# A spectral mixing layer with a routed feed-forward on one core: sine halves compared after the cosine rows, and one conditional store

## The chip, the cores and the metric

The kernel runs on one core of a Trainium2 chip. The metric is device microseconds of one execution. The kernel before takes 200.77 us, the median of three runs (200.58 to 201.01).

## The reference, cut to what matters

```python
x = A_x                                                   # 2048 tokens x 576, float32
h = x + _A_ref(_layernorm(x), seq_re, seq_im, hid_re, hid_im)
h2 = h + _B_ref(_layernorm(h), w_r, w_gate, w_up, w_down)

def _A_ref(x, dft_seq_re, dft_seq_im, dft_hid_re, dft_hid_im):
    a = jnp.einsum("bsd,ed->bse", x, dft_hid_re)
    b = jnp.einsum("bsd,ed->bse", x, dft_hid_im)
    return jnp.einsum("ts,bse->bte", dft_seq_re, a) - jnp.einsum("ts,bse->bte", dft_seq_im, b)

def _B_ref(x, w_r, w_gate, w_up, w_down):
    r = x @ w_r                                           # one score per token
    idx = jnp.argsort(-r, axis=-1)[:, :1]                 # the best token alone
    g, u = _silu(x_sel @ w_gate), x_sel @ w_up            # 576 -> 4608
    y = ((g * u) @ w_down) * _sigmoid(r_sel)              # 4608 -> 576
    return x + scatter(y at idx)
```

The two sequence matrices are 2048 x 2048 and arrive as inputs, as do the hidden matrices (576 x 576) and the three weights of the feed-forward (4608 x 576 each). Everything is float32. One token gets the feed-forward; all others get h plus its layer norm.

## The kernel before, in words

**Slots and tiles.** Token t lies on partition t // 16 in slot t mod 16, so X holds 16 slots of 128 x 576. A row of tiles of the cosine matrix (i = 0) or the sine matrix (i = 1) belongs to one slot j and is loaded as a tile of nine blocks of 128 x 128 (576 KB). Cosine and sine are symmetric, so the kernel multiplies with folded inputs and needs only the rows 0 to 8, in two groups: group zero of the list GROUPS is rows 1 to 5 (called group one in the change's title), the other is rows 6, 7, 0 and 8. Buffers: D0, D1 and D2 for the rows that are multiplied (five, five and four tiles), and a ring of seven tiles R, joined by the D tiles that are free at the time, for what is only compared.

**Comparisons.** Since the matrices are inputs, the kernel may only fold them if they really are symmetric. It reads the whole of both and compares. `off_h` (line 387) compares the two halves of each block of the rows in D, in two operations for each call; `off_s` (line 375) compares a tile with its mirrored part and `off_t` (line 380) a tile with that of row 16 - j. VectorE (DVE) writes the differences as bf16 into one of two slots of the buffer Q, ScalarE (ACT) squares and sums them (line 368), and at the end a sum that is not zero branches into a general version of the whole computation. With these inputs it is not taken. The mirrored parts come as gathers that GpSimd issues (POOL, line 301); all other loads are issued by SP in a fixed order (line 357 for the tiles, 403 and 405 for the hidden matrices W, 1173 and 1175 for the weights of the feed-forward). A load into a ring tile waits until the comparisons that read the tile's former content are done, and what stands behind it on its queue waits too.

**Around them.** PE multiplies the folded input XF with the rows in five blocks (line 565); ACT copies one part (579) and DVE keeps the result in Z (583). PE then multiplies Z with W (610), DVE adds the residual (619) and takes the router's score (623), ACT the variance (630). When all scores are there, the token is found, its slot is brought to all partitions, and the feed-forward runs as products and sums on POOL (1201), DVE (1190, 1197) and ACT (1206), with the last product on PE (1228). ACT stores the token's row last (1251).

**Stores of the other rows.** `STORE_RUNS` lists runs of slots (first slot, count) that POOL stores when the results of the batch that holds the run's first slot are there (lines 667 and 669). `LATE_RUNS` are two runs, slots 4 to 8 and slot 0, that SP stores under a condition, in two places (line 1052): early, behind the first feed-forward loads, if the token lies in one of those slots, and otherwise behind the last load. `other_rows` (lines 1040 to 1046) works out the two flags on POOL.

**What sets the order.** Python writes each step into a list with an engine, an estimated duration and the steps it depends on. `Plan.order` then runs through the list: at each point an engine takes, of the steps that are ready, the one with the longest way to the end. The instructions of each engine are emitted in that order, and an engine never departs from it. `qs.take()` hands out the two slots of Q in the order in which the steps are written down. In the part that the change touches, the order of writing is: halves of group zero in three portions (rows 1 and 2, rows 3 and 4, row 5), each with its cosine and sine tiles in one slot of Q and one square (2304, 2304 and 1152 elements wide); then `c_check` for cosine rows 1 to 5; then the five blocks on PE.

Of the kernel before, what the change touches and what calls it, by code (L numbers as in the profile page):

```python
# [7 lines left out]
F32 = mybir.dt.float32  # L8
# [3 lines left out]
OP = mybir.AluOpType  # L12
AX = mybir.AxisListType

P = 128
# [22 lines left out]
GROUPS = [[1, 2, 3, 4, 5], [6, 7, 0, 8]]  # L38
# [4 lines left out]

HALVES = [[(0, 2), (2, 2), (4, 1)], [(0, 2), (2, 2)]]

STORE_RUNS = [(1, 3), (13, 3), (11, 2), (9, 2)]
LATE_RUNS = [(4, 5), (0, 1)]

X_RUNS = [(0, 2), (14, 16), (2, 6), (6, 10), (10, 14)]

# [2 lines left out]
HM = P // 2  # L53
# [17 lines left out]
class Plan:  # L71
# [6 lines left out]
    def add(self, eng, dur, fn, *deps, tail=0.0, push=0.0):  # L78
        flat = []
        for d in deps:  # L80
            flat += d if isinstance(d, list) else [d]
        n = {"eng": eng, "dur": dur, "fn": fn, "deps": [d for d in flat if d], "tail": tail, "push": push}
        n["i"] = len(self.ops)
        self.ops.append(n)
        return n
# [57 lines left out]
def kernel(  # L143
# [13 lines left out]
    pe, act, dve, pool, sp = nc.tensor, nc.scalar, nc.vector, nc.gpsimd, nc.sync  # L157

    consts = ctx.enter_context(tc.tile_pool(name="consts", bufs=1))
    small = ctx.enter_context(tc.tile_pool(name="small", bufs=3))  # L160
# [132 lines left out]
    ov = out.rearrange("(p k) d -> p k d", k=NK)  # L293
# [11 lines left out]
    X = mp.tile([P, NK, D], F32, name="X")  # L305
# [10 lines left out]
    Q = QT.bitcast(BF16).rearrange("p (n w) -> p n w", n=2)  # L316
# [62 lines left out]
        o = Q[:, u % 2, 14 * P : QW].rearrange("p (k m) -> p k m", m=P)  # L379
        dve.tensor_tensor(o, C[NK - j, i, False], C[j, i, False][:, :, ::-1], op=SIGN[i])  # L380

    def off_h(g, c, n, i, u):

        o = Q[:, u % 2, i * 9 * n * HM : (i + 1) * 9 * n * HM].rearrange("p (c k m) -> p c k m", k=9, m=HM)
        t = DT[g, i][:, c : c + n]
        for k, op in enumerate((OP.subtract, OP.add)):
            dve.tensor_tensor(o[:, :, k::2, :], t[:, :, k::2, 0:HM], t[:, :, k::2, HM:P], op=op)  # L387
# [208 lines left out]
    def slots_of(j):  # L596
        return [j, NK - j] if j in PAIRS else [j]
# [86 lines left out]
    add = plan.add  # L684

    def then(f, *args):
        return lambda: f(*args)
# [20 lines left out]
    def in_turn(eng, f, mb, *deps):  # L708
        LAST[eng], d = load(eng, f, mb, LAST[eng], *deps)
        return d  # L710

    IDENT = []
    for k, n in X_LOADS:
        d = in_turn("SP" if k < 9 else "POOL", then(load_x, k, n), 0.295 * n)
# [11 lines left out]
    for a, b in X_RUNS:  # L726
# [4 lines left out]
        m = [add("ACT", 0.95, then(measure, k), f, push=push) for k, f in zip(ks, r)]  # L731
        o = add("POOL", 0.3, then(totals, a, b), e, m)
# [3 lines left out]
        o = add("POOL", 2.0, then(biases, a, b), r, o)  # L736
# [6 lines left out]
    users = {b: [] for b in ["XF", "Z", "Q", "WA", "WB", "WC", *range(N_RAW)]}  # L743
# [16 lines left out]
    for k in FOLDED:  # L760
        dg, use, at = [], [], []
        for sl in slots_of(k):
            n = next(places)
            UF[sl] = LATER[n]
            at.append(PLACE[n])
            if k in PAIRS:
                u, w = dgs.take()
                dg.append(add("DVE", 0.17, then(diag, sl, u), MEAS[sl], w, IDENT))
                use.append(u)
        if k in PAIRS:  # L770
            of = ys if k % 2 else zs
# [30 lines left out]
    CU = {}  # L802

    def c_load(j, i, mirror):
        CU[j, i, mirror] = ring("POOL" if mirror else "SP", load_c, 0.46 if mirror else 0.59, j, i, mirror)
# [8 lines left out]
            LAST["SP"], d = load("SP", then(load_c, None, j, i, False), 0.59, w, LAST["SP"])  # L814
            CU[j, i, False] = u, d

    def c_half(g, c, m):
        u, w = qs.take()
        cus = [[CU[j, i, False] for j in GROUPS[g][c : c + m]] for i in range(2)]
        n = [  # L820
            add("DVE", 0.16 + 0.62 * m, then(off_h, g, c, m, i, u), [d for _, d in cus[i]], w)
            for i in range(2)
        ]
        for i in range(2):
            for b, _ in cus[i]:
                users[b].append(n[i])
        squares(u, 9 * m * P, n)

    def squares(u, w, n, ps=P):
        SQUARES.append(add("ACT", 0.3 + w / 1200, then(square, u, w, ps), n))  # L830
        qs.users[u].append(SQUARES[-1])

    def c_check(j, i):

        u, w = qs.take()
        u0, d0 = CU[j, i, False]
        c_load(j, i, True)
        u1, d1 = CU[j, i, True]
        n = [add("DVE", 1.08, then(off_s, j, i, u, 0), d0, d1, w)]
        users[u0] += n  # L840
        users[u1] += n
        free.append(u1)
        if j in PAIRS:
            m = NK - j
            c_load(m, i, False)
            c_load(m, i, True)
            (u2, d2), (u3, d3) = CU[m, i, False], CU[m, i, True]
            n.append(add("DVE", 1.08, then(off_s, m, i, u, 1), d2, d3, w))
            users[u3].append(n[1])
            n.append(add("DVE", 1.36, then(off_t, j, i, u), d0, d2, w))  # L850
            users[u0].append(n[2])
            users[u2] += n[1:]
            free.extend([u3, u2])
        if u0[0] == "D1":
            free.append(u0)
        squares(u, QW if j in PAIRS else 7 * P, n)
# [28 lines left out]
    def seq_step(g, n):  # L885
        nonlocal pe_last
        w = len(GROUPS[g]) * HM
        (z0, w0_), (z1, w1_) = zs.take(), zs.take()
        need = [CU[j, i, False][1] for i in PARTS[n] for j in GROUPS[g]]
        pe_last = add("PE", 9 * w * 0.00171, then(seq, g, n), need, FOLDS, w0_, w1_, pe_last)  # L890
        for i in PARTS[n]:
            for c in range(len(GROUPS[g])):
                users[D_TAG[g, i], c].append(pe_last)
        users["XF"] = [pe_last]
        SEQ[g, n] = pe_last, z0, z1

    def keep_step(g, n):
        w = len(GROUPS[g]) * HM
        pe, z0, z1 = SEQ[g, n]
        u, wo = odds.take()  # L900
        h = add("ACT", 0.11 + 0.00085 * w, then(keep, g, n, 0), pe, wo)
        l = add("DVE", 2 * (0.07 + 0.00106 * w), then(keep, g, n, 1), h, ZU.get((g - 1, n > 0), []))
        odds.users[u].append(l)
        zs.users[z0].append(l)
        zs.users[z1].append(h)
        KEPT.setdefault(g, []).append(l)
# [22 lines left out]
    def batch(js):  # L929
# [6 lines left out]
        for k in [k for j in js for k in slots_of(j)]:  # L936
            if k in (0, 8):
                RESULTS.append(add("POOL", 1.3, then(result_on_pool, k), f, push=push + 5.0))
            else:
                RESULTS.append(add("ACT", 0.79, then(result, k), f, push=push))  # L940
        for k, n in STORE_RUNS:
            if k in [q for j in js for q in slots_of(j)]:
# [8 lines left out]
        for b in [b for b in free if type(b) is tuple and b[0] == tag]:  # L951
            free.remove(b)

    for c, m in HALVES[0]:
        c_half(0, c, m)
    for j in GROUPS[0][:3]:
        c_check(j, 0)
    w_first()
    for j in GROUPS[0][3:]:
        c_check(j, 0)  # L960
    for n in (0, 1, 4, 2, 3):
        seq_step(0, n)
        keep_step(0, n)
# [18 lines left out]
    for i in range(2):  # L982
        for j in GROUPS[1]:
            c_check(j, i)
    for c, m in HALVES[1]:
        c_half(1, c, m)
    for c in range(2):
        hid_step(0, c)
    for n in (0, 1):
# [12 lines left out]
    T = {}  # L1002
# [32 lines left out]

    def other_rows():

        s = small.tile([1, 3], F32, tag="near", name="near", bufs=1)
        T["late"] = small.tile([1, 2], I32, tag="late", name="late", bufs=1)
        pool.tensor_scalar(s[:, 0:1], T["ci"][0:1, 1:2], LATE_RUNS[0][0] - 0.5, None, op0=OP.is_ge)  # L1040
        pool.tensor_scalar(s[:, 1:2], T["ci"][0:1, 1:2], sum(LATE_RUNS[0]) - 0.5, None, op0=OP.is_le)
        pool.tensor_scalar(s[:, 2:3], T["ci"][0:1, 1:2], 0.5, None, op0=OP.is_le)
        pool.tensor_tensor(s[:, 0:1], s[:, 0:1], s[:, 1:2], op=OP.mult)
        pool.tensor_tensor(s[:, 0:1], s[:, 0:1], s[:, 2:3], op=OP.add)
        pool.tensor_scalar(T["late"][:, 0:1], s[:, 0:1], 1.0, 0.0, op0=OP.mult, op1=OP.add)
        pool.tensor_scalar(T["late"][:, 1:2], s[:, 0:1], -1.0, 1.0, op0=OP.mult, op1=OP.add)

    def store_if(n):

        on = sp.value_load(T["late"][0:1, n : n + 1], min_val=0, max_val=1)  # L1050
        for k, m in LATE_RUNS:
            st = sp.dma_start(ov[:, k : k + m, :], X[:, k : k + m, :], cond=on)
            tc.declare_no_dep(st.ins, group="spread", reason="stores of different rows")
            tc.add_to_no_dep_group("direct", st.ins)
            if n == 1:
                tc.declare_no_dep(st.ins, group="kept", reason="stores that only one of two conditions lets run")
                tc.add_to_no_dep_group("late", st.ins)
            else:
                tc.add_to_no_dep_group("kept", st.ins)

    def to_all():
        ph = T["ph"] = ypair("ph")
# [29 lines left out]
    rows = add("DVE", 0.55, T["steps"][4], most)  # L1092
# [3 lines left out]
    near = add("POOL", 1.0, other_rows, slot, push=50.0)  # L1096
# [26 lines left out]
    o = add("DVE", 1.0, check_sum, SCORES, SQUARES, xs_is)  # L1123
    o = add("PE", 0.3, check_all, o)
# [6 lines left out]
    for b in range(NJ // TW):  # L1131
        j = TW * b
# [112 lines left out]
    def late_part():  # L1245
        T["mv"] = nc.values_load(T["miss"][0:1, 0:1], min_val=0, max_val=1)
        store_if(1)
# [13 lines left out]
    def plan_ffn(after):  # L1261
# [41 lines left out]

        load_to(N_BUF)
        LAST["SP"] = add("SP", 1.5, then(store_if, 0), near, RESULTS, LAST["SP"])
        for b in range(NJ // TW):
            j = TW * b
# [23 lines left out]
    with tc.If(T["mv"], preferred_fallthrough_block=False):  # L1331
        with ExitStack() as gen:
# [33 lines left out]
            with ExitStack() as hs:  # L1366
# [9 lines left out]
                with tc.For_i(0, NK, 1) as k:  # L1376
                    dve.tensor_copy(xr, row_of(GX, k))
                    norm(xn, xr, "x")
                    for a in range(5):
                        w = min(P, D - a * P)  # L1380
# [4 lines left out]
                    for c in range(4):  # L1385
                        pa = zbank(f"gpa{c}")
                        for a in range(5):
                            w = min(P, D - a * P)
# [39 lines left out]
            key, ci = steps[5]()  # L1428
# [75 lines left out]
```

## Time and profile before

| | |
|---|---|
| median of three runs | 200.77 us |
| profiled execution | 201.27 us |
| its span | 199.2 us |
| DVE busy | 166.1 us (83%) |
| ACT busy | 140.5 us (71%) |
| PE busy | 130.4 us (65%) |
| POOL busy | 122.8 us (62%) |
| moved by DMA | 77.81 MB, mean 391 GB/s |

A row of a timeline gives start, duration, engine, line, operation, result<-inputs, how many instructions are merged in it (xN), and in brackets how long the engine stood idle before it and what ended that. A row of waits gives who waited for whom: microseconds in total, times, the longest. In a table of stretches each engine's busy time stands in its column, then the granted clock of PE, the mean busy share of the 16 DMA engines, and GB/s. The page's slices are 1/40 of the span, about 5 us each; a digit is the busy share in tenths.

### The profile page before, as it was taken

What the parts mean: (1) busy time and instruction counts of PE and PEld (TensorE: products, weight loads), DVE (VectorE), ACT (ScalarE), POOL (GpSimd) and SP (SyncE); (2) the same over time, 40 slices, a digit from 0 to 9 for tenths busy, and PEclk for the clock granted to TensorE, in tenths of its full rate; (3) what the DMA queues carried; (4) which work ended last, traced back from release to release, by engine and by line L of the source; (5) the groups of instructions that cost most, each with busy time, mean ns of one, the idle gap of its engine ahead of it and who ended that gap; (6) DMA issues with size and microseconds to landing.
All of it is one profiled execution on the core that took longest, in us unless ns stands there. A gap on an engine that the chain in (4) does not pass through costs nothing. (4 is left out here: it accounts for less than half of the span.)

```text
span 199.2 us, 2787 instructions
## 1 busy us (share of the span) xinstructions
PE 130.4 (65%) x758; PEld 89.9 (45%) x758; DVE 166.1 (83%) x419; ACT 140.5 (71%) x259; POOL 122.8 (62%) x134
## 2 busy tenths in 40 slices
PE   0007989999999989899999996600241444085840
PEld 0005667764767778677877774400121111043220
DVE  4389997989999859997999999999839997899410
ACT  2298863783987794799587599997629999786400
POOL 6578888495528878998870000006439999998500
PEclk9999999999999999999999999985555555555798
DMA  5999999999979999999999999999999999999991
GB/s 190 361 418 415 411 411 409 409 372 346 402 275 366 415 398 391 404 407 412 407 401 418 420 420 422 427 414 423 422 428 425 428 422 420 431 420 412 422 387 42
DMA packets 14491, 77.81 MB, mean 391 GB/s; under 512 B 1855, under 2 KB 1859, under 8 KB 11143
## 3 DMA queue, kind: packets, MB, share of 16 engines
q1 hardware_dynamic: 10463, 56.56, 70.8%
q0 software_dynamic: 4000, 21.03, 26.3%
q8 instruction: 7, 0.11, 0.2%
q14 instruction: 13, 0.11, 0.1%
q10 hardware_dynamic: 8, 0.00, 0.0%
HBM read 72.86 MB, written 6.49 MB: 398 GB/s over the span
## 5 line engine op out<-in xcount | busy, mean ns | idle before, releaser
L368 ACT ACTIVATE Q<-Q 128x2944 bf16<-128x2944 bf16 (+5 forms) x26 | 55.4, 2133 | 19.9 <-DVE Q L375 7.0
L610 PE MATMUL py<-W,Z 128*128 128x289 f32 x180 | 45.3, 408 | 2.3 <-DVE X L619 2.3
L565 PE MATMUL ps<-D,XF 128*128 128x320 f32 (+3 forms) x216 | 45.0, 408 | 1.2 <-DMA D<-in_ct_dram 0.8
L301 POOL DMA_INDIRECT R<-in_ct_dram,ic x21 | 34.1, 1625 | 14.5 <-DVE Q L375 10.5
L610 PEld LDWEIGHTS py<-W,Z 128*128 128x128 f32 x180 | 33.7, 189 | 13.6 <-issue 2.9
L565 PEld LDWEIGHTS ps<-D,XF 128*128 128x128 f32 (+1 forms) x216 | 32.1, 172 | 13.8 <-issue 2.5
L1201 POOL TENSOR_TENSOR D<-D,Z 128x1152 f32<-128x1152 f32 x8 | 20.8, 2618 | 1.2 <-SPq L1331 1.2
L667 POOL DMA_DIRECT2D out_dram<-X x1 | 0.6, 606 | 30.0 <-ACT X L661 30.0
L301 POOL DMA_INDIRECT D<-in_ct_dram,ic x11 | 16.1, 1468 | 3.4 <-issue 2.4
L498 ACT ACTIVATE junk<-X,XT 128x576 bf16<-128x576 f32 x16 | 12.4, 772 | 8.0 <-DVE W L459 6.5
L1206 ACT ACTIVATE junk<-D 128x576 bf16<-128x576 f32 x20 | 13.7, 683 | 4.0 <-POOLq L1331 2.3
L1228 PE MATMUL pd<-XF,H 128*1 128x144 f32 x80 | 5.3, 440 | 16.1 <-DVE H L1220 13.3
L537 PE MATMUL fo<-W,diag 128*128 128x288 f32 (+1 forms) x8 | 3.9, 665 | 16.4 <-DVE diag L528 16.4
L387 DVE TENSOR_TENSOR Q<-D 128x640 bf16<-128x640 f32 (+3 forms) x20 | 12.7, 691 | 1.4 <-DMA D<-in_ct_dram 1.4
L380 DVE TENSOR_TENSOR Q<-R,D 128x1152 bf16<-128x1152 f32 x10 | 13.4, 1349 | 0.0
L630 ACT ACTIVATE junk<-X,TD 128x576 bf16<-128x576 f32 x16 | 12.3, 768 | 1.5 <-DVE X L619 1.3
L375 DVE TENSOR_TENSOR Q<-R,D 128x896 bf16<-128x896 f32 x11 | 11.9, 1083 | 1.3 <-DMA D<-in_ct_dram 1.2
L661 ACT ACTIVATE X<-X,BB,UP 128x576 f32<-128x576 f32 x14 | 10.8, 855 | 2.4 <-DVE BB L642 2.4
L623 DVE SCALAR_TENSOR_TENSOR junk<-X,wr 128x576 bf16<-128x576 f32 x16 | 12.1, 754 | 0.3
L375 DVE TENSOR_TENSOR Q<-D 128x896 bf16<-128x896 f32 x11 | 11.8, 1081 | 0.0
L619 DVE SCALAR_TENSOR_TENSOR X<-py,X 128x576 f32<-128x576 f32 x16 | 11.5, 748 | 0.0
L375 DVE TENSOR_TENSOR Q<-R 128x896 bf16<-128x896 f32 x10 | 10.8, 1084 | 0.7 <-DMA R<-in_ct_dram,ic 0.7
(202 smaller groups left out, 262.5 us busy)
## 6 DMA issues: line engine op xcount, KB each, us to landing
D<-in_ct_dram SPq DMA_DIRECT2D x22, 576.0 KB
R<-in_ct_dram SPq DMA_DIRECT2D x10, 576.0 KB
D<-in_wu_dram SPq DMA_DIRECT2D x5, 1152.0 KB
D<-in_wd_dram SPq DMA_DIRECT2D x4, 1152.0 KB
R<-in_wg_dram SPq DMA_DIRECT2D x3, 1152.0 KB
D<-in_wg_dram SPq DMA_DIRECT2D x3, 1152.0 KB
out_dram<-X SPq DMA_DIRECT2D x2, 1440.0 KB
X<-in_x_dram SPq DMA_DIRECT2D x4, 576.0 KB
```

What stands on the lines that cost most here:

```text
L301: pool.indirect_dma_start(tile, None, view, bass.IndirectOffsetOnAxis(ap=rows, axis=0), element_offset=at)
L368: act.activation(t, t, AF.Square, accum_out=DS[0 : t.shape[0], n : n + 1])
L375: dve.tensor_tensor(o, C[j, i, True][:, 0:7, :], C[j, i, False][:, 7:0:-1, :], op=SIGN[i])
L380: dve.tensor_tensor(o, C[NK - j, i, False], C[j, i, False][:, :, ::-1], op=SIGN[i])
L387: dve.tensor_tensor(o[:, :, k::2, :], t[:, :, k::2, 0:HM], t[:, :, k::2, HM:P], op=op)
L498: act.activation(junk[:, 0:D], X[:, k, 0:D], AF.Square, bias=XT[:, n : n + 1], scale=-float(D), accum_out=VX[:, n : n + 1],)
L565: pe.matmul(cm(ZP[g, n][k % 2][p0 : p0 + m], w), XF[:, q, m0 : m0 + m], DT[g, i][:, :, k, 0:HM], start=k in (0, 1), stop=k in (6, 7),)
L610: pe.matmul(YP[GROUPS[g][c]][:, h, 0:w], Z[:, a, c * P : (c + 1) * P], w_block(a)[:, h * HD : h * HD + w], start=(a == 0), stop=(a == 4),)
L623: dve.scalar_tensor_tensor(junk2, X[:, k, 0:D], 1.0, wr, op0=OP.mult, op1=OP.mult, accum_out=TD[:, n, 0:1])
L630: act.activation(junk[:, 0:D], X[:, k, 0:D], AF.Square, bias=TD[:, n, 1:2], scale=-float(D), accum_out=VAR[:, n : n + 1],)
L1201: pool.tensor_tensor(t, t, xs.unsqueeze(1).to_broadcast([P, JW, D]), op=OP.mult)
L1206: act.activation(junk[:, 0:D], WB[w, j][:, r, :], AF.Copy, accum_out=acc[:, j + r : j + r + 1])
```

## The change

Two things are rewritten. First, group zero's halves become one portion of all five cosine tiles (one slot of Q, one square 2880 wide), written down first, and one of all five sine tiles, written down after the five cosine rows' `c_check`. The halves of the other group stay as they are. Second, the late runs become one, slots 3 to 8, still under the condition and in the same two places; slots 0 to 2 become an unconditional run in `STORE_RUNS`, which now starts with slot 0 and so belongs to the last batch of results. The flags need two operations less.

```diff
-STORE_RUNS = [(1, 3), (13, 3), (11, 2), (9, 2)]
-LATE_RUNS = [(4, 5), (0, 1)]
+STORE_RUNS = [(0, 3), (13, 3), (11, 2), (9, 2)]
+LATE_RUN = (3, 6)
...
-    def off_h(g, c, n, i, u):
-
-        o = Q[:, u % 2, i * 9 * n * HM : (i + 1) * 9 * n * HM].rearrange("p (c k m) -> p c k m", k=9, m=HM)
+    def off_h(g, c, n, i, u, at):
+
+        o = Q[:, u % 2, at : at + 9 * n * HM].rearrange("p (c k m) -> p c k m", k=9, m=HM)
...
-    def c_half(g, c, m):
+    def halves(g, parts, ms):
         u, w = qs.take()
-        cus = [[CU[j, i, False] for j in GROUPS[g][c : c + m]] for i in range(2)]
-        n = [
-            add("DVE", 0.16 + 0.62 * m, then(off_h, g, c, m, i, u), [d for _, d in cus[i]], w)
-            for i in range(2)
-        ]
-        for i in range(2):
-            for b, _ in cus[i]:
-                users[b].append(n[i])
-        squares(u, 9 * m * P, n)
+        n, at = [], 0
+        for i in ms:
+            for c, m in parts:
+                cus = [CU[j, i, False] for j in GROUPS[g][c : c + m]]
+                o = add("DVE", 0.16 + 0.62 * m, then(off_h, g, c, m, i, u, at), [d for _, d in cus], w)
+                for b, _ in cus:
+                    users[b].append(o)
+                n.append(o)
+                at += 9 * m * HM
+        squares(u, at, n)
...
-    for c, m in HALVES[0]:
-        c_half(0, c, m)
+    halves(0, HALVES[0], [0])
     for j in GROUPS[0][:3]:
         c_check(j, 0)
     w_first()
     for j in GROUPS[0][3:]:
         c_check(j, 0)
+    halves(0, HALVES[0], [1])
...
-    for c, m in HALVES[1]:
-        c_half(1, c, m)
+    for part in HALVES[1]:
+        halves(1, [part], [0, 1])
...
-        pool.tensor_scalar(s[:, 2:3], T["ci"][0:1, 1:2], 0.5, None, op0=OP.is_le)
...
-        pool.tensor_tensor(s[:, 0:1], s[:, 0:1], s[:, 2:3], op=OP.add)
...
-        for k, m in LATE_RUNS:
-            st = sp.dma_start(ov[:, k : k + m, :], X[:, k : k + m, :], cond=on)
+        k, m = LATE_RUN
+        st = sp.dma_start(ov[:, k : k + m, :], X[:, k : k + m, :], cond=on)
```

The planner then sets other orders. On DVE, where the first mirrored comparison stood behind four portions of halves, these rows stand in the kernel before (D holds the rows in D0 and D1, fo is a fold of the input, R the ring; a number behind 128x counts what the operation covers; in brackets the semaphores it waits for):

```order
L387 TENSOR_TENSOR Q<-D 128x2x5x64 [waits DMAHW6_49,DMAHW5_49]
L387 TENSOR_TENSOR Q<-D 128x2x4x64
L548 TENSOR_SCALAR XF<-fo_370 128x287 [waits Activation_49]
L387 TENSOR_TENSOR Q<-D 128x2x5x64 [waits DMAHW7_49]
L387 TENSOR_TENSOR Q<-D 128x2x4x64
L387 TENSOR_TENSOR Q<-D 128x2x5x64 [waits DMAHW4_49,DMAHW3_49]
L387 TENSOR_TENSOR Q<-D 128x2x4x64
L375 TENSOR_TENSOR Q<-R,D 128x896 [waits DMASW4_49,Activation_49]
L375 TENSOR_TENSOR Q<-R 128x896 [waits DMAHW0_49,DMASW5_49,DVE_49]
L380 TENSOR_TENSOR Q<-R,D 128x1152
L387 TENSOR_TENSOR Q<-D 128x5x64 [waits DMAHW2_49,Activation_49]
L387 TENSOR_TENSOR Q<-D 128x4x64 [waits DVE_49]
```

and in the changed kernel, from the same place:

```order
L387 TENSOR_TENSOR Q<-D 128x2x5x64 [waits DMAHW1_49,DMAHW0_49]
L387 TENSOR_TENSOR Q<-D 128x2x4x64
L548 TENSOR_SCALAR XF<-fo_370 128x287 [waits Activation_49]
L375 TENSOR_TENSOR Q<-R,D 128x896 [waits DMASW4_49]
L387 TENSOR_TENSOR Q<-D 128x5x64 [waits DMAHW2_49]
L387 TENSOR_TENSOR Q<-D 128x4x64
L375 TENSOR_TENSOR Q<-R 128x896 [waits DMAHW0_49,DMASW5_49]
L380 TENSOR_TENSOR Q<-R,D 128x1152
L724 TENSOR_SCALAR bt<-tf 128x16
```

The first mirrored comparison (L375) has moved ahead of the last cosine portion, and no sine tile is read here.

The sine halves stand further down on DVE, behind the comparisons of cosine row 5 (the first, fourth and fifth rows here) and between the keeps of the blocks (L583):

```order
L375 TENSOR_TENSOR Q<-R,D 128x896 [waits DMASW4_49,Activation_49]
L583 SCALAR_TENSOR_TENSOR Z<-ps_4_0_435,sgn,os_4_476 128x5x64 [waits Activation_49]
L583 SCALAR_TENSOR_TENSOR Z<-ps_4_0_435,sgn,os_4_476 128x5x64
L380 TENSOR_TENSOR Q<-R,D 128x1152 [waits DMAHW0_49]
L375 TENSOR_TENSOR Q<-R 128x896 [waits DMASW5_49,DVE_49]
L583 SCALAR_TENSOR_TENSOR Z<-ps_2_0_464,os_2_501 128x5x64 [waits Activation_49]
L583 SCALAR_TENSOR_TENSOR Z<-ps_2_0_464,os_2_501 128x5x64
L387 TENSOR_TENSOR Q<-D 128x2x5x64 [waits DMAHW4_49,DMAHW3_49,DVE_49]
L387 TENSOR_TENSOR Q<-D 128x2x4x64
L387 TENSOR_TENSOR Q<-D 128x2x5x64 [waits DMAHW6_49,DMAHW5_49]
L387 TENSOR_TENSOR Q<-D 128x2x4x64
```

In the kernel before, the keep with sgn stood ahead of the first of these rows, and the second comparison of row 5 ahead of the sum with row 11 (L380). The order of issues on SP is the same in both kernels up to the first conditional store, and the order on PE is the same throughout.

On POOL the run of slots 0 to 2 moves, as the piece of the difference between the two orders shows:

```order
 L301 DMA R<-in_ct_dram,ic 128x896
 L301 DMA D<-in_ct_dram,ic 128x896 x2
-L667 DMA out_dram<-X 128x1728
-L677 MEMSET tick 1x1
 L669 DMA out_dram<-X,ix 128x9216
 L677 MEMSET tick 1x1
```

It now stands behind the flags (lines 1041 to 1045 of the changed kernel) and the two results that POOL itself works out.

More of the change, by code (lines that the diff above doesn't have):

```diff
@@ L1036, in other_rows @@
     def other_rows():
-        s = small.tile([1, 3], F32, tag="near", name="near", bufs=1)
+        s = small.tile([1, 2], F32, tag="near", name="near", bufs=1)
         T["late"] = small.tile([1, 2], I32, tag="late", name="late", bufs=1)
-        pool.tensor_scalar(s[:, 0:1], T["ci"][0:1, 1:2], LATE_RUNS[0][0] - 0.5, None, op0=OP.is_ge)
-        pool.tensor_scalar(s[:, 1:2], T["ci"][0:1, 1:2], sum(LATE_RUNS[0]) - 0.5, None, op0=OP.is_le)
-        pool.tensor_scalar(s[:, 2:3], T["ci"][0:1, 1:2], 0.5, None, op0=OP.is_le)
+        pool.tensor_scalar(s[:, 0:1], T["ci"][0:1, 1:2], LATE_RUN[0] - 0.5, None, op0=OP.is_ge)
+        pool.tensor_scalar(s[:, 1:2], T["ci"][0:1, 1:2], sum(LATE_RUN) - 0.5, None, op0=OP.is_le)
         pool.tensor_tensor(s[:, 0:1], s[:, 0:1], s[:, 1:2], op=OP.mult)
-        pool.tensor_tensor(s[:, 0:1], s[:, 0:1], s[:, 2:3], op=OP.add)
         pool.tensor_scalar(T["late"][:, 0:1], s[:, 0:1], 1.0, 0.0, op0=OP.mult, op1=OP.add)
@@ L1050, in store_if @@
         on = sp.value_load(T["late"][0:1, n : n + 1], min_val=0, max_val=1)
-        for k, m in LATE_RUNS:
[L1052 to L1059, printed above, removed]
+        k, m = LATE_RUN
+        st = sp.dma_start(ov[:, k : k + m, :], X[:, k : k + m, :], cond=on)
+        tc.declare_no_dep(st.ins, group="spread", reason="stores of different rows")
+        tc.add_to_no_dep_group("direct", st.ins)
+        if n == 1:
+            tc.declare_no_dep(st.ins, group="kept", reason="stores that only one of two conditions lets run")
+            tc.add_to_no_dep_group("late", st.ins)
+        else:
+            tc.add_to_no_dep_group("kept", st.ins)
     def to_all():
```

## The prediction

> **What bounds the kernel now.** I read the page's slices first, then the busy time by stretch, then the queue of loads and what holds it back.
>
> ```profile
> DMA  5999999999979999999999999999999999999991
> ...
> core 0: us, PE busy (x) PEld busy (x) DVE busy (x) ACT busy (x) POOL busy (x), PEclk, DMA share, GB/s
> 44.00:48.00 4.00, 4.00 (x32) 1.89 (x28) 3.68 (x4) 1.76 (x5) 1.99 (x2) 1.00 1.05 302
> 56.00:60.00 4.00, 4.00 (x15) 2.43 (x15) 4.00 (x6) 3.59 (x4) 1.61 (x1) 1.00 0.73 249
> 60.00:65.00 5.00, 5.00 (x21) 3.86 (x21) 5.00 (x7) 3.77 (x6) 4.39 (x3) 1.00 0.99 369
> 76.00:100.00 24.00, 23.48 (x101) 18.86 (x101) 22.81 (x36) 18.71 (x24) 21.23 (x10) 1.00 1.02 408
> 130.00:190.00 60.00, 21.16 (x238) 10.61 (x238) 49.50 (x162) 45.39 (x111) 43.79 (x31) 0.54 1.01 422
> ```
>
> The DMA engines are the bound: their share is 1.0 nearly throughout, and no compute engine is full after 130 us. The time is therefore bytes over rate, plus the places where the queues fall short, plus the tail. Two such places lie in the middle. From 44 to 48 us only 302 GB/s move, yet the engines are busy (1.05): slow, not starved. From 56 to 60 us they are starved: share 0.73, 249 GB/s. Against a full share that costs (1 - 0.73) x 4 = 1.08 us; against 408 GB/s it costs (408 - 249) x 4 / 408 = 1.56 us.
>
> The tail starts from the last weights:
>
> ```profile
> 172.97 0.33 SPq L1175 DMA_DIRECT2D W<-in_wd_dram  x1
> 175.71 3.14 SPq L1052 DMA_DIRECT2D out_dram<-X  x2
> ...
> 192.24 1.16 PE L1228 MATMUL pd<-W,H 128*1 128x144 f32 x32 [0.94 <-SPq L1331]
> 193.47 0.37 DVE L1241 SCALAR_TENSOR_TENSOR orow<-pd,sg,orow 97x144 f32<-97x144 f32 x1 [3.79 <-PE pd L1228]
> 193.98 1.37 ACTq L1251 DMA_DIRECT2D out_dram<-orow  x1
> ```
>
> The last weight load is issued at 172.97 and PE has work on W only at 192.24, some 19 us later: the queue holds that much in front. So whatever moves the stream of loads forward at 60 us, and is not lost again, moves the end by as much.
>
> Why is the queue empty at 57 us? SP issues in order and stands behind DVE:
>
> ```profile
> SPq L357 <- DVE Q L375: 17.3, 4, 7.1
> ...
> 48.98 0.33 SPq L357 DMA_DIRECT2D R<-in_ct_dram  x1
> ...
> 57.14 0.33 SPq L357 DMA_DIRECT2D R<-in_ct_dram  x1
> 57.52 2.78 SPq L357 DMA_DIRECT2D D<-in_ct_dram  x5
> ...
> 56.03 1.09 DVE L375 TENSOR_TENSOR Q<-R,D 128x896 bf16<-128x896 f32 x1
> ```
>
> After 48.98 SP issues nothing for 8 us. The load at 57.14 waits for the comparison that ends at 56.03 + 1.09 = 57.12 (cosine row 5, which frees its buffer), and five loads of 576 KB stand behind it.
>
> **The change part by part.** *The sine halves.* Before that comparison DVE does both halves of all five rows:
>
> ```profile
> 30.57 1.42 DVE L387 TENSOR_TENSOR Q<-D 128x640 bf16<-128x640 f32 x2
> ...
> 33.71 1.43 DVE L387 TENSOR_TENSOR Q<-D 128x640 bf16<-128x640 f32 x2 [1.36 <-DMA D<-in_ct_dram]
> ...
> 35.42 2.75 DVE L387 TENSOR_TENSOR Q<-D 128x640 bf16<-128x640 f32 x4
> ...
> 41.37 1.56 DVE L387 TENSOR_TENSOR Q<-D 128x320 bf16<-128x320 f32 x4
> ...
> 44.32 1.36 DVE L380 TENSOR_TENSOR Q<-D 128x1152 bf16<-128x1152 f32 x1 [0.52 <-ACT Q L368]
> 52.84 1.00 DVE L583 SCALAR_TENSOR_TENSOR Z<-ps,sgn,os 128x320 f32<-128x320 f32 x2
> ```
>
> Halves: 1.42 + 1.43 + 2.75 + 1.56 = 7.16 us; the sine's share, 3.58, now comes after the comparison. So does the keep of the fifth block (52.84 to 53.76, 0.92). The wait of 1.36 for a sine tile goes, since only cosine tiles are read at that point, and I take the 0.52 wait for a square as gone too. I charge 1.0 us for new small waits (a fold's copy that ACT must finish, a square that frees the buffer Q), between 0 and the 1.88 removed. The comparison would end at 57.12 - 3.58 - 0.92 - 1.88 + 1.0 = 51.7.
>
> One thing is then late: the sum of cosine row 4 against its mirror needs a tile loaded behind W:
>
> ```profile
> 35.11 0.34 SPq L357 DMA_DIRECT2D D<-in_ct_dram  x1
> ...
> 16.91 0.33 SPq L357 DMA_DIRECT2D D<-in_ct_dram  x1
> ...
> 54.76 1.35 DVE L380 TENSOR_TENSOR Q<-D 128x1152 bf16<-128x1152 f32 x1
> ```
>
> DVE would ask for it three operations earlier (1.35 + 1.08 + 1.09, less overlap), near 48.4; before, it read it at 54.76 without waiting. When does it land? The load issued at 16.91 released DVE at 33.71, 16.8 us in the queue; the same wait gives 51.9. I take 51, between 48.4 (no cost) and 51.9, which is an estimate, and DVE stalls 2.6 us. The comparison ends at 54.3 and the load follows, 2.8 us earlier than 57.14. The spell begins within the 56 to 60 us above, near 56.5, and the first bytes come one to two us after an issue, so nearly all of it fills: **-1.4 us**, between -1.08 and -1.56. The weak 60 to 65 us (369 GB/s) may mend too: (408 - 369) x 5 / 408 = 0.5, taken as 0. The slow 44 to 48 us are engine-bound: 0, at best -(408 - 302) x 4 / 408 = -1.04.
>
> *What the moved work holds up.* POOL's gathers feed the other queue, and the page of waits does not name what blocks this one:
>
> ```profile
> 60.51 0.94 POOL L301 DMA_INDIRECT R<-in_wt_dram,iw  x1 [0.30 <-DVE Z L583]
> 61.75 5.58 POOL L301 DMA_INDIRECT D<-in_wt_dram,iw  x1 [0.30 <-issue]
> 67.63 1.43 POOL L301 DMA_INDIRECT D<-in_wt_dram,iw  x1 [0.30 <-issue]
> ...
> 60.90 1.08 DVE L375 TENSOR_TENSOR Q<-R,D 128x896 bf16<-128x896 f32 x1
> ...
> 65.43 1.09 DVE L375 TENSOR_TENSOR Q<-R,D 128x896 bf16<-128x896 f32 x1
> 67.20 1.09 DVE L375 TENSOR_TENSOR Q<-R 128x896 bf16<-128x896 f32 x1 [0.68 <-DMA R<-in_ct_dram,ic]
> ```
>
> A gather that takes 0.94 us at 60.51 takes 5.58 at 61.75: it spans DVE's unbroken comparisons and ends 0.8 us after the gap that begins at 66.52. In the change DVE runs, from 54.3: three keeps (0.9 each), two comparisons (1.35 + 1.0), the sine halves (3.58), then the same six comparisons (68.29 - 60.90 - 0.68 = 6.7) with no gap for data, to 69.6. The gather would end near 70.4, 3.1 us later than at 67.33. Does that starve the queues? From 56.5 us there are six loads of 590 KB, two more once the comparisons free their buffers, and three gathers of 459, 459 and 590 KB: 6.2 MB, or 15.2 us at 408 GB/s, so work until 71.7. The late gather's bytes come one to two us after its end, about then. I charge **+0.4 us**, between 0 and the whole +3.1.
>
> The Trainium skill (SBUF — State Buffer, section "SBUF: two separate sides") calls the port pair that VectorE and GpSimd share an exclusive lock, held for the whole instruction, also by VectorE operations with two SBUF inputs against a GpSimd operation that reads SBUF. The trace agrees that gathers are held, but here one was not released at four ends of operations between 61.75 and 66.43. By the rule alone a gather would lose one operation at most, this term would be 0 and the sum -1.4.
>
> *ACT* squares two tiles of 2880 instead of 2304, 2304 and 1152: one fixed cost less, worth nothing while DVE feeds it. *PE* runs the same order:
>
> ```profile
> 70.57 8.01 PE L565 MATMUL ps<-D,XF 128*128 128x256 f32 x36 [0.77 <-DMA D<-in_ct_dram]
> ```
>
> Its last block of group one needs the banks that the keep of 52.84 frees, which now ends near 54.3 + 0.9 = 55.2 instead of 53.76. PE starts 1.4 us later there, of which the 0.77 us that it waits for loads at 70.57 takes a part: 0 while DVE sets the pace, at worst +0.7.
>
> *The stores.*
>
> ```profile
> 134.62 0.61 POOL L667 DMA_DIRECT2D out_dram<-X  x1 [30.01 <-ACT X L661]
> ...
> 149.68 2.62 POOL L1201 TENSOR_TENSOR XF<-XF,Z 128x1152 f32<-128x1152 f32 x1 [2.90 <-ACT Z L1076]
> ```
>
> The store of three slots goes from 134.62 to behind the flags, about 145. Its 0.7 us on POOL lies in the 2.90 us that POOL waits for the token's row; without that cover it would cost 0.7. The DMA engines stay full from 130 to 190 us, so the order of bytes changes, not their sum. One conditional store replaces two (3.14 us between issues), but both stand behind 19 us of queue: 0, between -0.2 and +0.2. Slots 3 to 8 are six, as 4 to 8 and 0 were. The reference's router picks row 1922 = 16 x 120 + 2, slot 2, which is in neither late set, so 1.77 MB are still stored at the end.
>
> Sum: -1.4 + 0.4 = -1.0. The profiled execution took 201.27 (span 199.2 and 2.07 around it) and would take 200.3; it lies 0.50 above the median of 200.77, so the median becomes **199.8**.
>
> **The rivals.** *The lead is used up (200.8).* The loads from 90 us on are issued when DVE or PE frees a buffer; if these are no earlier, the queue that is ahead just empties at another place. For it: DVE is busy 22.81 of 24 us from 76 to 100, and the moved 3.58 us must still be done. Against it: its idle time there, and the 0.68 before 67.20, are waits for DMA, which shrink as loads come earlier.
>
> *Gathers held behind DVE (202.5, slower).* It is the mechanism of 61.75, at that place: DVE has over eleven us without a gap, POOL issues in order, and one late gather holds those behind it, while SP's next loads wait for the same comparisons. For it: four ends of operations let no gather through. Against it: any wait for data is a gap, so the hold ends by itself once DVE runs dry. It decides when the gather ends later than about 70, since the queues have work until 71.7. Price: the whole 3.1 against the 1.4 won, +1.7.
>
> *The slow stretch mends too (198.2).* Gathers come earlier and run beside the slow loads at 44 to 48: -1.56 - 1.04 = -2.6. Against it: the share there is already 1.05.
>
> *The change doesn't do what it says:* the planner could have put the halves elsewhere; the order of DVE shows them moved. A token in slots 3 to 8 would store early and delay the last weights by 1.77 MB / 422 GB/s = 4.2 us; the router's row excludes it.
>
> **How the numbers follow.** A run of this kernel can tell about 0.2% (0.4 us) from no change. Forecast 0.44, lead used up 0.24, gathers held 0.18, slow stretch mends 0.14. Faster: all of the last, and 0.41 of the forecast: 0.55. Same: 0.03 of the forecast and most of the used-up lead: 0.25. Slower: 0.18 and 0.02 of it: 0.20. The forecast's own range is 199.1 to 200.5; the range for 8 in 10 reaches into both outer cases and leaves about a tenth out at either end: 198.4 to 201.7.
>
> **What would show it.** Right: in 56 to 60 us over 380 GB/s, the load of 57.14 at 53.5 to 55.5, the slices after 60 us full, the last weights' PE work about 1 us before 192.24. Wrong: a new hole at 70 to 78 us, gathers of over 4 us between 60 and 70, or DVE waiting for the row-4 tile until after 53. If the spell fills and the end does not move, the lead was used up, and the stretch that shows a share below 1.0 names where.

## The result, and the profile after

The changed kernel takes **203.67 us** (median of five runs, 202.80 to 204.19), the kernel before on the same chip 200.94 us (200.58 to 201.18): a ratio of **1.0136, 95% interval 1.0107 to 1.0166**. Forecast was 199.8. The profiled execution took 202.80 with a span of 201.0; it is the fastest of the five, so its trace shows the smaller part of the loss. (Some kernels further down scatter by some per cent from run to run: a median there is over all runs, a ratio over those within 1.5% of the kernel's fastest.)

The stretches of the changed kernel, columns as in the prediction:

```profile
44.00:48.00 4.00, 4.00 (x31) 1.91 (x27) 4.00 (x6) 3.01 (x4) 1.55 (x1) 1.00 1.03 394
48.00:52.00 4.00, 4.00 (x17) 2.89 (x16) 0.48 (x1) 1.94 (x3) 0.00 (x0) 1.00 1.04 332
52.00:56.00 4.00, 2.15 (x8) 1.17 (x7) 0.82 (x1) 0.00 (x0) 0.00 (x0) 1.00 0.87 349
56.00:60.00 4.00, 0.48 (x1) 0.48 (x2) 4.00 (x6) 2.37 (x1) 1.55 (x1) 0.70 0.19 36
60.00:65.00 5.00, 5.00 (x12) 3.10 (x12) 5.00 (x8) 3.74 (x8) 2.69 (x2) 0.56 0.98 388
```

The dry spell from 56 to 60 us isn't filled; it is deeper: share 0.19 and 36 GB/s, where there were 0.73 and 249. From 48.5 to 55.2 us VectorE stands idle (the two stretches from 48 to 56 us show 0.48 and 0.82 us of work in four each), and GpSimd does nothing. Who waits for whom stands in the timelines of VectorE, SP and GpSimd (start, duration, engine, line, operation; in brackets the idle time before it and what ended it):

```profile
47.40 1.08 DVE L375 TENSOR_TENSOR Q<-D 128x896 bf16<-128x896 f32 x1
55.18 1.36 DVE L380 TENSOR_TENSOR Q<-D 128x1152 bf16<-128x1152 f32 x1 [6.70 <-DMA D<-in_ct_dram]
56.45 2.09 DVE L375 TENSOR_TENSOR Q<-R,D 128x896 bf16<-128x896 f32 x2
...
35.45 0.34 SPq L357 DMA_DIRECT2D D<-in_ct_dram  x1
39.29 19.61 SPq L357 DMA_DIRECT2D R<-in_ct_dram  x3
58.95 2.44 SPq L357 DMA_DIRECT2D D<-in_ct_dram  x5
...
57.81 1.55 POOL L301 DMA_INDIRECT R<-in_ct_dram,ic  x1 [10.31 <-DVE Q L375]
```

The tile in question is the one that line 380 compares with cosine row 4: that of row 12, which SP loads behind W (issued at 35.45). It is called the row-4 tile below. VectorE is ready for it at 47.40 + 1.08 = 48.5 and starts on it at 55.18. The two comparisons behind it end at 58.54; only then does SP get out the third load of its group (ends at 58.90) and the five behind it, and GpSimd's next gather has stood for 10.31 us. Both queues hang on one tile.

The price in bytes, from the queue view of 30 to 100 us, first of the kernel before, then of the changed one:

```profile
DMA packets 6232, 27.09 MB, mean 387 GB/s; under 512 B 870, under 2 KB 870, under 8 KB 6229
```
```profile
DMA packets 6068, 26.29 MB, mean 376 GB/s; under 512 B 855, under 2 KB 855, under 8 KB 6065
```

0.80 MB fewer, at the 408 GB/s of full stretches 1.96 us. The end, in the chain of waits:

```profile
193.93 1.20 PE pd L1227 x32
195.16 0.37 DVE orow L1240
```

PE starts on the last weights at 193.93 instead of 192.24 and `orow` is at 195.16 instead of 193.47: 1.69 us later each. From 65 to 185 us both kernels keep the engines full (shares of 1.01 to 1.03), so the bytes are not won back. The hole at 55 to 60 us accounts for the end of this execution; the medians lie 2.73 us apart, and no trace of one of the longer runs of this kernel was kept.

### The profile page after: what moved, and what is told of

It is laid out like the page before. It is cut to its first block, busy times and chain, and to the rows that moved or that the text cites. A ratio compares the mean times of both kernels' runs of the same rounds, so it can differ in the third digit from the quotient of the medians.

```text
span 201.0 us, 2780 instructions
## 1 busy us (share of the span) xinstructions
PE 131.9 (66%) x758; PEld 91.2 (45%) x758; DVE 166.5 (83%) x419; ACT 140.6 (70%) x257; POOL 112.3 (56%) x132
## 5 line engine op out<-in xcount | busy, mean ns | idle before, releaser
L565 PE MATMUL ps<-D,XF 128*128 128x320 f32 (+3 forms) x216 | 47.3, 420 | 5.4 <-DVE Z L583 5.4
L610 PE MATMUL py<-W,Z 128*128 128x289 f32 x180 | 44.8, 408 | 0.2 <-DVE X L619 0.2
L565 PEld LDWEIGHTS ps<-D,XF 128*128 128x128 f32 (+1 forms) x216 | 33.6, 179 | 18.6 <-DVE Z L583 5.9
L301 POOL DMA_INDIRECT R<-in_ct_dram,ic x21 | 29.0, 1382 | 22.1 <-DVE Q L375 18.3
L669 POOL DMA_INDIRECT out_dram<-X,ix x3 | 3.1, 1037 | 35.5 <-DVE junk L623 33.4
L301 POOL DMA_INDIRECT D<-in_ct_dram,ic x11 | 13.2, 1201 | 7.6 <-DVE Q L380 4.6
L380 DVE TENSOR_TENSOR Q<-R,D 128x1152 bf16<-128x1152 f32 x10 | 13.4, 1350 | 0.0
L375 DVE TENSOR_TENSOR Q<-R,D 128x896 bf16<-128x896 f32 x11 | 11.8, 1083 | 1.0 <-DMA D<-in_ct_dram 1.0
L375 DVE TENSOR_TENSOR Q<-D 128x896 bf16<-128x896 f32 x11 | 11.8, 1083 | 0.0
L375 DVE TENSOR_TENSOR Q<-R 128x896 bf16<-128x896 f32 x10 | 10.8, 1087 | 0.8 <-DMA R<-in_ct_dram 0.8
```

The lines of the kernel that those rows point to most:

```text
L301: pool.indirect_dma_start(tile, None, view, bass.IndirectOffsetOnAxis(ap=rows, axis=0), element_offset=at)
L375: dve.tensor_tensor(o, C[j, i, True][:, 0:7, :], C[j, i, False][:, 7:0:-1, :], op=SIGN[i])
L565: pe.matmul(cm(ZP[g, n][k % 2][p0 : p0 + m], w), XF[:, q, m0 : m0 + m], DT[g, i][:, :, k, 0:HM], start=k in (0, 1), stop=k in (6, 7),)
L610: pe.matmul(YP[GROUPS[g][c]][:, h, 0:w], Z[:, a, c * P : (c + 1) * P], w_block(a)[:, h * HD : h * HD + w], start=(a == 0), stop=(a == 4),)
```

## The experiments

**One part alone.** The kernel before with the halves moved and the old stores; then with the new stores and the old halves:

```
-    for c, m in HALVES[0]:                    # halves alone
-        c_half(0, c, m)
+    halves(0, HALVES[0], [0])                 # cosine; the sine half follows the checks
 
-STORE_RUNS = [(1, 3), (13, 3), (11, 2), (9, 2)]   # stores alone
-LATE_RUNS = [(4, 5), (0, 1)]
+STORE_RUNS = [(0, 3), (13, 3), (11, 2), (9, 2)]
+LATE_RUN = (3, 6)
```

> Only the halves are moved; the stores are those of the kernel before. Theory 1 (the late tile): VectorE, freed of 3.58 us of sine halves, asks for the cosine's row-4 tile at 48.5 us and gets it only near 55, SP's next load stands behind that comparison, and both queues run dry from 55 to 60. Then this kernel shows the whole loss: 203.0 to 204.0 us, a wait of 6 to 7 us on VectorE at 48 to 55, under 100 GB/s from 56 to 60. Theory 2 (the stores): the store of slots 0 to 2 and the one conditional store cost part of the 2.7 us. Then this kernel stands at 201.5 to 202.7.

> Only the stores are changed; the halves stand as in the kernel before. Theory 1: no difference, 200.6 to 201.2 us, since the DMA engines are full from 130 to 190 us whatever the order of bytes. Theory 2: 0.7 to 1.3 us slower, 201.6 to 202.2, with the last weights landing later or a store after them ending later.

Measured: the halves alone 203.46 us, ratio 1.0099 (1.0068 to 1.0129); the stores alone 201.36 us beside 201.25 for the kernel before, ratio 0.9996 (0.9972 to 1.0021). With the halves alone the page of waits has

```profile
DVE Q L380 <- DMA D<-in_ct_dram: 7.1, 1, 7.1
```

The loss comes with the halves, and the stores cost nothing that can be measured. Theory 2 falls. This profile is of a longer execution (203.99 us) and has the larger hole: 28 GB/s from 56 to 60 us, 26.11 MB from 30 to 100 us, and PE's work on the last weights at 195.08, 2.84 us later than in the kernel before.

**Why is the tile late?** Two things stand in its way: W's loads in front of it on SP's queue, and the gathers on the other queue. First W, loaded behind cosine rows 4 and 5 in the changed kernel, and the same in the kernel before:

```
     for j in GROUPS[0][:3]:
         c_check(j, 0)
-    w_first()
     for j in GROUPS[0][3:]:
         c_check(j, 0)
+    w_first()
```

> The changed kernel with W's four loads (1.37 MB) moved behind the loads of the cosine's rows 4 and 5. Theory 1: the row-4 tile no longer stands behind W, and lands some 4 us earlier (1.37 MB at the 343 GB/s of that stretch), near 51; the comparison of row 5 ends near 54.5 instead of 58.5, W is still in the queue then, and the dry spell is gone: 199.3 to 200.5 us, faster than both kernels. If it is only the gathers beside it that make the tile late, it still lands after 53.5 and the time is above 202.

> The kernel before (halves and stores as they were) with W's four loads behind the loads of the cosine's rows 4 and 5. Theory 1: in the kernel before VectorE has no wait before the comparison that ends at 57.12, so an earlier tile frees nothing: 200.6 to 201.3 us, and the share from 56 to 60 us stays below 0.85. If it is the place of W alone that costs, it is as fast as the kernel with W moved and the halves moved, 199.3 to 200.5.

Measured: 203.53 us, ratio 1.0117 (1.0087 to 1.0147), with the halves moved; 200.93 us, ratio 0.9990 (0.9966 to 1.0015), with the old halves. The time of the first was missed, but the place behaves as said. Its stretches, and its VectorE later on:

```profile
48.00:52.00 4.00, 4.00 (x17) 2.84 (x16) 4.00 (x5) 3.09 (x4) 3.30 (x1) 1.00 1.05 396
52.00:56.00 4.00, 4.00 (x17) 2.81 (x16) 4.00 (x7) 2.23 (x5) 3.41 (x2) 1.00 1.02 285
56.00:60.00 4.00, 4.00 (x16) 2.50 (x15) 3.10 (x6) 2.95 (x5) 3.90 (x1) 1.00 1.03 408
100.00:130.00 30.00, 26.24 (x127) 18.91 (x126) 29.58 (x50) 22.64 (x37) 4.14 (x3) 1.00 0.88 347
...
92.50 1.08 DVE L375 TENSOR_TENSOR Q<-R,D 128x896 bf16<-128x896 f32 x1
100.39 1.09 DVE L375 TENSOR_TENSOR Q<-R,D 128x896 bf16<-128x896 f32 x1 [6.80 <-DMA D<-in_ct_dram]
```

There is no wait for row 4 any more, 56 to 60 us run at 408 GB/s, and the gain is thrown away at 93.6 us by a wait of 6.80 us for another tile, with a share of 0.88 after 100 us. The prediction's "lead used up" is here, in a kernel that has a lead. In the kernel with the old halves SP's load behind the row-5 comparison still goes out at 57.2 (in the kernel before 57.14), and the stretch there is

```profile
56.00:60.00 4.00, 4.00 (x16) 2.43 (x15) 4.00 (x6) 3.50 (x4) 1.52 (x1) 1.00 0.95 334
```

Its share is above the 0.85 expected, but not because W is still in the queue: SP's queue moves 0.53 MB there, in packets of 4.4 KB, and the kernel before 0.54; the gathers move 0.80 MB instead of 0.45. There is no gain in time that can be measured.

**The gathers.** What each queue moved from 44 to 48 us (q0 GpSimd's, q1 SP's: packets, MB, share of the engines), before and after:

```profile
q1 hardware_dynamic: 391, 1.19, 104.3%
q0 software_dynamic: 2, 0.01, 0.9%
```
```profile
q0 software_dynamic: 205, 1.13, 71.6%
q1 hardware_dynamic: 206, 0.45, 31.4%
```

In the kernel before, SP's queue had the engines to itself in these 4 us, with the end of W and the tiles behind it; after, gathers are there as well, and the two queues get as many packets, 205 and 206. But W's packets are small (0.45 MB / 206 = 2.2 KB) and the gathers' large (5.5 KB), so SP's queue gets 0.45 MB instead of 1.19. The Trainium skill (DMA: Bandwidth & Descriptors, section "Queues, rings and completion order") says that an engine takes turns between the queues that have work, a packet at a time. The counts of these 4 us agree, if the profile counts as a packet what the Trainium skill calls one; those from 40 to 43 us of the run with W moved, 156 of the gathers and 71 of SP's, do not show equal turns. The gathers are earlier since VectorE, rid of the sine halves, frees the ring sooner, and since one that was stuck is not: the row at 39.45 of the kernel before is the same gather as that at 37.77 of the changed one.

```profile
39.45 4.29 POOL L301 DMA_INDIRECT R<-in_ct_dram,ic  x1 [2.39 <-DVE Q L375]
```
```profile
37.77 1.04 POOL L301 DMA_INDIRECT R<-in_ct_dram,ic  x1 [0.30 <-issue]
```

To try it, one operation on a single element keeps back the two gathers that nothing needs yet; the orders of all engines stay as they are (in short):

```
+    pool.tensor_scalar(held, DS[0:1, n : n + 1], 1.0, 0.0, op0=OP.mult, op1=OP.add)   # n: the sum of cosine row 3's square
     gather(...)                                                                         # sine row 1
```

> The changed kernel; on GpSimd one small operation ahead of the gather of sine row 1 waits for the square of cosine row 3 (ends at 49.5 us), so the two gathers issued at 42.88 and 45.95, which nothing needs before 61 us, come after 49.5. All other orders are the same. Theory 1a (gathers that run ahead take the engines' time from the tile that VectorE waits for): two gathers of 459 KB fewer ahead of the row-4 tile, 2.2 to 2.5 us, so it lands at 52.3 to 53.3 instead of 55.1, SP's load goes out at 55.7 to 56.7 instead of 58.57, the hole shrinks by 2 us and the time is 201.2 to 202.6, unless a later wait takes it back. Theory 1b (W's slow loads alone make the tile late): it lands at 54.5 to 55.5 as before, and the gathers come later for nothing: 203.5 to 205.5.

Measured: median 202.12 us (twelve runs, 200.35 to 206.60); ratio 1.0001 (0.9975 to 1.0027). In its profile (200.95 us; code lines are one higher):

```profile
49.91 0.18 POOL L840 TENSOR_SCALAR held<-DS 1x1 f32<-1x1 f32 x1 [5.94 <-ACT Q L369]
...
53.21 1.36 DVE L381 TENSOR_TENSOR Q<-D 128x1152 bf16<-128x1152 f32 x1 [4.44 <-DMA D<-in_ct_dram]
...
56.98 2.46 SPq L358 DMA_DIRECT2D D<-in_ct_dram  x5
...
56.00:60.00 4.00, 2.45 (x5) 1.67 (x6) 4.00 (x6) 3.17 (x7) 1.39 (x1) 0.70 0.69 227
```

VectorE starts on the tile at 53.21 instead of 55.18 (expected 52.3 to 53.3), five loads go out at 56.98 instead of 58.95, and 56 to 60 us are back at 227 GB/s. From 30 to 100 us this profile moves 27.16 MB, the kernel before 27.09, the changed one 26.29 and that with the halves alone 26.11; their spans are 199.2, 199.2, 201.0 and 202.0 us, so in these traces the time follows the missing bytes. An operation that does no work and only delays GpSimd gives the loss back in seven of the twelve runs (200.35 to 202.24); the other five took 203.44 to 206.60, and the median keeps about 1 us of the loss. So gathers that run ahead are a cause; theory 1b falls as the whole story. W's place in front is the other part, shown by the run that moved it.

**The second place.** With W moved, the wait at 93.6 should be the same fault. In the kernel before, VectorE waits little for that tile:

```profile
94.58 1.09 DVE L375 TENSOR_TENSOR Q<-R,D 128x896 bf16<-128x896 f32 x1 [1.19 <-DMA D<-in_ct_dram]
```

What the queues moved from 80 to 94 us, in the kernel before and in that with W moved:

```profile
q1 hardware_dynamic: 819, 3.39, 60.7%
q0 software_dynamic: 414, 2.32, 40.8%
```
```profile
q0 software_dynamic: 542, 3.13, 55.2%
q1 hardware_dynamic: 638, 2.61, 47.1%
```

The gathers gained 0.81 MB and SP's tiles lost 0.78. Two holds there, strong, and then weaker (in words, against the kernel with W moved; each holds a gather until the square named has ended):

```
+    hold gather of row 7, cosine          until the square of sine row 4    # strong
+    hold gather of row 0, cosine          until the square of sine row 5
 
+    hold gather of row 7, cosine          until the square of sine row 3    # weaker
+    hold gather of row 9, cosine          until the square of sine row 4
```

> The changed kernel with W behind rows 4 and 5, and two small operations on GpSimd that hold the gathers of row 7 until the square of sine row 4 is done (about 87 us) and those of rows 0 and 8 until that of sine row 5 (about 95). Theory 1a: with W moved, the wait of 6.80 us on VectorE at 93.6 is the same fault at a second place (11 gathers landed from 80 to 100 us, where the kernel before had 8, and the tile issued at 79.88 took 20.4 us); held back, the tile lands by 94.5, the wait is under 2.5 us, the share from 100 to 130 us is 0.97 or more, and the lead of some 1.9 us stays: 198.8 to 200.5 us. Rival: VectorE's work up to the router sets the end, and with the holds the gathers themselves come late: 201.5 to 203.5.

> As the kernel with W behind rows 4 and 5 and the gathers held, but held less: row 7's first gather until the square of sine row 3 (about 82.5 us), its second until that of sine row 4 (about 88), nothing after. Theory 1a: the gathers then come where those of the kernel before came (its own were stuck until 87.9 and 92.5), the tile that released VectorE at 100.39 without a hold releases it at 94 to 97, neither queue runs dry, and the time is 199.5 to 201.5. Rival: there is no middle, what one queue gains the other lacks, since both streams are needed by the same comparisons: 202 to 204.

> The kernel with W behind rows 4 and 5 and the weaker hold once more, on another occasion, since two of its six runs were near 204. If the time is a property of the order, most runs lie at 199.3 to 199.8 again and the ratio to the kernel before at 0.990 to 0.994; if the four were luck, the median is above 201.

Measured, strong: median 205.72 us (201.27 to 207.15), a miss. The wait of 6.80 us is gone, but the queues ran dry: the rival had the late gathers, though not the size (201.5 to 203.5).

```profile
86.00:100.00 14.00, 14.00 (x61) 11.18 (x60) 12.46 (x17) 10.30 (x13) 8.03 (x6) 1.00 0.86 331
```

Weaker: median 199.59 us, ratio **0.9921 (0.9901 to 0.9942)** from four of the six runs, the lowest median of all. Its profile:

```profile
56.00:60.00 4.00, 4.00 (x16) 2.45 (x15) 3.65 (x7) 3.57 (x5) 3.80 (x1) 1.00 1.03 411
86.00:100.00 14.00, 14.00 (x63) 11.53 (x62) 10.14 (x13) 7.27 (x10) 11.07 (x10) 1.00 1.03 412
100.00:130.00 30.00, 25.58 (x123) 18.32 (x121) 29.86 (x60) 25.41 (x42) 0.30 (x1) 1.00 1.01 420
...
94.19 1.09 DVE L376 TENSOR_TENSOR Q<-R,D 128x896 bf16<-128x896 f32 x1 [3.86 <-DMA D<-in_ct_dram]
```

The tile comes at 94.19 instead of 100.39, and no stretch is starved. But on the second occasion the median was 202.88, above the 201.40 of the kernel before beside it, and the ratio of 0.9945 (0.9899 to 0.9991) is that of four of its ten runs. Of the sixteen runs of both, seven lie at 199.43 to 199.62 and nine at 201.89 to 205.21. It can beat the kernel before by 0.8%, and does so in fewer than half of its runs.

The second occasion left a profile of 205.21 us. Beside that of 199.62 it shows where such a run of the same kernel loses; the quicker one first:

```profile
ACT W L416 <- DMA W<-in_wt_dram: 2.0, 2, 1.2
...
82.18 0.59 POOL L840 TENSOR_SCALAR held<-DS 1x1 f32<-1x1 f32 x1 [2.58 <-ACT Q L369]
```
```profile
ACT W L416 <- DMA W<-in_wt_dram: 3.7, 2, 2.8
...
90.58 0.18 POOL L840 TENSOR_SCALAR held<-DS 1x1 f32<-1x1 f32 x1 [15.98 <-ACT Q L369]
...
86.00:100.00 14.00, 14.00 (x60) 11.01 (x59) 11.02 (x15) 11.43 (x16) 6.07 (x7) 1.00 0.66 244
```

In the longer run VectorE is 1 us behind at 48.5 us; W, which now lies behind rows 4 and 5, lands later, and ScalarE, which stands for it, goes on at 57.91 instead of 55.36. From there the delay grows: VectorE's keep is 2.56 us later (62.19 instead of 59.63), PE waits 6.38 us for a tile instead of 1.49, and the square that opens the first hold ends so late that GpSimd stands for 15.98 us and both queues run dry. Opened so late, the weaker hold is as long as the strong one. The hold need not be the whole of it: the last kernel of this section runs dry in the same stretch without one, in its profile of 206.44 us (219 GB/s). What starts the delay isn't settled.

**Do the moved halves have any worth?** The same two edits with the halves and stores of the kernel before:

> The kernel before (old halves, old stores) with W behind rows 4 and 5 and the same two holds as in the fastest kernel so far. Theory 2 (the moved halves are worth something once the tile no longer waits behind W): without them the row-5 comparison still ends near 57, the two edits alone do not fill 56 to 60 us, and the time is 200.5 to 201.5. Rival: the two edits make the gain by themselves, and the moved halves have no worth: 199.3 to 200.0.

Measured: median 202.69 us (200.69 to 205.45), ratio 1.0041 (1.0002 to 1.0081). No gain without the moved halves, not even in the quickest run (200.69, where the kernel with the moved halves reached 199.43); 56 to 60 us stay short:

```profile
56.00:60.00 4.00, 4.00 (x15) 2.48 (x14) 3.89 (x6) 3.38 (x5) 1.82 (x1) 1.00 0.84 289
```

The time is above what was expected, so only the direction supports theory 2.

**Two that tell little.** The sine halves written ahead of rows 4 and 5, and, with W moved, the load of row 10 put ahead of the four sine tiles:

```
     w_first()
+    halves(0, HALVES[0], [1])                 # ahead of rows 4 and 5
     for j in GROUPS[0][3:]:
         c_check(j, 0)
-    halves(0, HALVES[0], [1])
 
     no_more("D0")
+    c_check(6, 0)                             # loads row 10's tile; left out of the loop behind it
     c_first(1, 1)
```

> The changed kernel with the sine halves written ahead of cosine rows 4 and 5 instead of behind them. Theory 1: 3.58 us of VectorE's work stand again where the tile is waited for, the wait falls from 6.7 to 1 to 3 us, and the row-5 comparison ends at 57 to 58: 200.6 to 202.0. If the two-portion squares or their slots are the cause, it stays at 203 to 204.

> The changed kernel with W behind rows 4 and 5, and the load of row 10 of the cosine (the tile waited for at 93.6 us) put ahead of the four sine tiles of group two in SP's order; the planner then also moves some of VectorE's steps. Theory 1a: the tile has four loads of 590 KB fewer in front of it and comes some 6 to 12 us earlier, so there is no wait of over 3 us on VectorE between 88 and 101, and the time is 199.0 to 201.5. Rival: the wait moves to TensorE and the sine tiles behind it, and the time is 202 to 204.

Measured: 207.03 us, ratio 1.0260 (1.0234 to 1.0286), and 203.10 us (200.39 to 206.44), ratio 1.0031 (0.9991 to 1.0070). Both missed. In both the planner moved many other steps of VectorE, so neither is an edit of one thing. The halves did not fill the first one's wait: in its profile (212.98 us, its longest run) VectorE still stands 5.36 us for the tile, until 56.29, where 1 to 3 us were expected, and the dry spell reaches 65 us (87 GB/s from 56 to 60, 208 from 60 to 65). Why it is so much slower stays open.

## Why the prediction was wrong, point by point

**The bound: right.** The kernel is bound by its loads, and what the stream loses at 60 us arrives at the end: 1.96 us of bytes, 1.69 us at the end.

**When VectorE asks: right.** Forecast 48.4, measured 48.5. The sum of removed halves holds.

**When the tile comes: the step that failed.** I took 51, between 48.4 and 51.9, and a stall of 2.6 us; it was 55.18 and 6.70 us. The 51.9 came from another load's time in the queue (16.8 us), as if that time belonged to the queue. It hangs on what else is in the queues. For the old order the estimate was good: the completion events of this load in the trace of before end at 50.5. But the change itself moves the gathers, and I priced the tile with the gathers where they had been; in the changed kernel its events end at 55.1. The row at 54.76, quoted in the same place, was the only bound from above that the trace gave: read there without a wait, so landed by then. With it the stall goes up to 54.76 - 48.4 = 6.4 us, the comparison ends near 58, later than in the kernel before, and the fall to the slower side would have been inside the working.

**The spell that fills, -1.4: wrong sign,** as a consequence; the forecast load of 53.5 to 55.5 went out at 58.57. The run with W moved shows that the spell does fill (408 GB/s) once the tile isn't late.

**Gathers held behind VectorE, +0.4, at worst +3.1: the wrong way round.** From 57 to 70 us the longest gather takes 2.77 us. Here a gather that comes later helps, as the held ones showed: it leaves the engines to the tile that VectorE needs. I feared that a gather would be held; the loss came from gathers that ran ahead, one of them because it no longer was. The rival of that name had the right side, and a price (202.5) that is 1.2 us short, but not the mechanism; that it came nearer than the forecast is luck. The Trainium skill's lock of the shared port (SBUF — State Buffer, section "SBUF: two separate sides"), which I had weighed there, was tried by itself in no run, so its part stays open.

**The slow 44 to 48 us, 0 (rival: mends, -1.04).** It did rise, from 302 to 394 GB/s, and nothing was gained: the added bytes are the gathers', W's come later, and 48 to 56 us run at 332 and 349. Where W goes, the slow stretch goes (285 GB/s at 52 to 56 with W moved).

**The lead used up (200.8): not in the change,** which never had a lead, but in the run with W moved, by a mechanism that I had not named: the same one, at 93.6 us.

**PE, 0 to +0.7.** It waits 5.4 us from 54 to 59.5, since VectorE's keep stands behind the late tile; it is behind the same cause.

**The stores, 0: right** (0.9996).

## What to carry to other kernels

Where two queues feed one engine in order, a load's time in its queue is no constant of the queue: when a change lets the other queue run ahead, price each waiting load again with that traffic beside it, and count packets as well as bytes. Before counting on an engine that gets free earlier, find the next thing that it asks for, and take as the latest arrival what the trace proves ("read here without a wait"), not a neighbour's latency. An accidental delay can be what keeps two streams in step; once it is gone, an explicit hold, or an order in which nothing urgent stands behind slow loads, has to take its place. A hold has a price of its own: where it opened late, the queues ran dry.

## What the runs showed of the hardware

- Two busy queues need not get equal bytes: from 44 to 48 us of the changed kernel they got 205 and 206 packets, but 1.13 and 0.45 MB. That the packets are always shared equally isn't shown (156 to 71 from 40 to 43 us with W moved).
- W's small packets are not slow by themselves: from 42 to 44 us of the kernel before, SP's queue has the engines almost to itself (342 of 355 packets, 2.2 KB each) and they move 388 GB/s. The 302 GB/s come after that, at 44 to 48 us, where W ends and the tiles behind it begin (391 packets of 3.0 KB); in the changed kernel and with W moved such a stretch lies at 48 to 52 and at 52 to 56 us (332 and 285 GB/s). What slows it stays open; larger pieces for W weren't tried.
- A gather isn't held by every unbroken run of VectorE: the one at 40.61 of the changed kernel, with VectorE busy without a gap from 39.25 to 48.48, took 1.82 us, that at 39.45 of the kernel before 4.29. What lets one through stays open.
- The kernel with the weaker hold lies anywhere from 199.43 to 205.21 us in sixteen runs, where the kernel before lies at 200.18 to 202.65 in the 21 runs beside the second ten and at 200.57 to 205.38 in the 15 beside the first six. In the two traces ScalarE's wait for W ends 2.55 us later, and the first hold opens 8.4 us later; whether the other runs go the same way wasn't tested.
